# A new order table for a fused attention and channel-mix kernel: first transfers, prices of landing and storing, and the stores ahead of the branch

## The chip, the core and the metric

The program runs on one core of a Trainium2 chip. The metric is the device time of one execution in microseconds (us); less is better. The core's engines work side by side, each through its own list of instructions in order: TensorE (PE in the profile; PEld is its weight load), VectorE (DVE), ScalarE (ACT), GpSimd (POOL) and SyncE (SP), which here only issues transfers. Waits between engines are semaphores. Transfers are issued by SP and, in a few places, by ACT.

## What is computed

Linear attention with softmax over features, then a channel mix with a gate. Cut to what matters:

```python
# q, k, v: (8 batches, 8 heads, 576, 64)
q_s = softmax(q, axis=-1)
k_s = softmax(k, axis=2)                       # over the sequence
kv  = einsum('bhsd,bhse->bhde', k_s, v)
x   = einsum('bhsd,bhde->bhse', q_s, kv)       # then (B, S, H*D) = (8, 576, 512)

x_prev = x shifted by one position, zeros in front
xk = mu_k * x + (1 - mu_k) * x_prev
xr = mu_r * x + (1 - mu_r) * x_prev
k  = maximum(xk @ w_k, 0)                      # w_k: 512 x 1024
v  = (k * k) @ w_v                             # w_v: 1024 x 512
out = sigmoid(xr @ w_r) * v                    # w_r: 512 x 512
```

## The kernel before

**Work.** A batch's eight heads are taken in two halves u = 0, 1 of four heads; `q b.u`, `k b.u`, `v b.u` are its loads (0.59 MB each). The steps of a batch, with the engine that runs them:

- `exp` of q and k on ACT (L332), cast of v to bf16 (L238), mostly on POOL; `sum_q` and `scale_q` on DVE (L342 to L347) normalise q.
- q is transposed: for batches 0 and 1 by TensorE (`turn_q`, L361), its result taken out of PSUM by two evictions; for later batches by a DMA transpose (L369).
- `kv` (L378) and, for batches 0 and 1, weighting by mu (`weigh_kv`, L393) and eight mixing steps `x_mixed` (L410), each evicted by ACT or DVE, that give xk and xr directly. For later batches `x` (L432), `shift_x` on ACT (L440) and `mix_x` on DVE (L445).
- `up b.f`, f = 0 to 7 (L454): xk times one eighth of w_k; `relu` on ACT (L459); `square` of a pair on DVE (L469) or ACT (L467).
- Two batches i = 0 to 3 together have nine tiles m of 128 rows: `gate i.m` (L473), `tanh` on ACT (L478), `down i.m` (L490), `finish` on DVE (L496) and `store` (L506), which issues two transfers, one for each half of the rows.

All three weights come in as f32 and are cast to bf16: w_k in two transfers (1.05 MB each) and eight casts, w_r in one transfer and two casts on POOL, w_v in two transfers and four casts. Every gate needs both casts of w_r, every `down` all four of w_v. The mixing weights mu are spread over the partitions by two small matmuls (`spread_mu`) and kept by ACT (`keep_mu`) and DVE (`keep_cols`).

**Order.** The order is set by a planner and a table. Each piece of work is a numbered step with an engine, a cost, a latency (`lat`, from its end to when others see it) and its predecessors. The table `ORDER` lists all 709 step numbers; a letter A, D or G puts a step with a choice of engines on ACT, DVE or POOL. `Plan.run` goes through the table, gives each step a start from the costs, and picks a buffer for each tile (the one that is free first by the plan). `Plan.emit` emits the steps by planned start; so each engine's list is the table cut down to that engine, and the costs decide only buffers, the merging of engines, and warm-up matmuls: `emit` fills TensorE's planned idle time from 2.0 us up to the step `up 0.0` with matmuls on the identity (L320), which keep its clock up. SP's list holds loads, DMA transposes and stores in one line, so a store that waits for its `finish` holds up what is behind it.

**The branch.** Softmax is computed without subtracting the maximum. A check of all row sums (`watch`, `gather`, `judge`, `read_flag`) decides on a branch (L793) whether a safe version of everything is computed again. The branch stands ahead of `down 3.7`, `down 3.8` (in two halves of the columns, a and b) and the finishing and storing of three tiles, 3.6, 3.7 and 3.8 (`TAIL`). All else is issued ahead of it. `landed` is a step without an instruction: it stands for the landing of all stores outside the tail. Of the tail's stores, both halves of 3.6 and the second halves of 3.7 and 3.8 are issued by ACT, the others by SP.

**Tiles on chip.** The loads have three buffers of each kind, `ot` (a tile's output) has four, the tail's outputs three; PSUM holds three two-bank buffers (`two`: transposes, kv, mixing, `up`) and two one-bank buffers (`one`: gate, down).

Of the kernel before, what the change touches and what calls it, by code (L numbers as in the profile page):

```python
# [18 lines left out]


ORDER = """
0 7 8 9 10 11 12 13 14 19 1 2 24 28 76 96 3 4 80 81 100 82 6 79G 77 84A 78G 101 83A 85 5 102 97
86 90 91A 87 98G 99G 103D 105 94 104D 95A 88 106 107 108 89A 110 112 109D 111A 113D 114 115D 17G
92 93D 27 18G 21D 367 368 22D 365 366 15A 29 20G 26 370 30 16D 31 23D 372 33 32 377 371 373 25
369D 536 136 378 116 375 34 537 374D 140 141 120 376 121 362 119G 360 526 117 531 361 527 118G
125 139G 363 137 532 142 122 124A 126 127 143A 521 123D 138G 145 37 40 43 130 144D 131A 134 146
148 135A 147 150 149A 151D 35G 128 154 129A 364D 152 153D 379D 38G 39D 41 380 155A 36G 42 45 381
522 156 397 159 387 382 383 160 388 173 46 161 523 524 176 385 386 157 389A 384D 44 177 538 539
528 158 398 529 162 163 132 133A 190 193 395 392 551 178 393 175 49 396 399D 552 530 533 174 194
534 164 561 165 390 166 541 167 170 55 48 192 391 562 179 47 168 546 169 180 394D 540 181 542  # L30
547 556 563 171 186 187 557 172 182 188 50 548 183 241 184 195 185 207 415 416 407 51 189 549
408 210 211 212 417 405 191 52 410 209 418 406 409A 196 564 411 576 197 400 208 244 565 245 577
535 402 401 403 571 198 419D 200 213 56 199 572 53 543 214 412 413 558 404D 550 201 202 204 57
544 414D 203 559 205 206 215 217 566 216 218 567 54 221 568 220 578 246 219 222 242 223 224 243
427 428 569 437 225 425 227 420 426 228 226 429D 247 545 438 421 581 430 431 579 586 582 58 587
248 249 251 230 250 231 591 229 592 422 252 553 423 255 583 254 570 253 257 258 232 580 59 560
256 237 435 238 584 233 436 64 554 573 424D 240 61 601 66 60 239 234 259 65 235 432 236 62 574
433 260 261 262 63 602 442 452 596 575 439D 443 275 440 441 606 292 450 453 294 278 434D 597 447
279 455 444D 295 263 608 585 451 293 280 264 456 607 298 299 555 277 609 448 525 265 445 276 598
266 446 449D 267 599 281 67 611 282 68 268 270 612 269 610 272 588 589 621 283 271 73 273 274 69  # L40
622 289 593 288 296 590 297 284 457 603 290 285 286 458 287 75 291 462 472 309 463 310 604 459D
626 594 595 470 627 473 74 471 467 616 311 454A 468 465 345 343 312 313 460 461 346 314 466 347
628 629 300 617 70 469A 301 315 316 302 304 305 303 344 613 614 475 615 646 306 72 647 308 476
71 464D 477 641 605 642 307 618 478 474D 479D 317 323 349 619 319 636 348 637 350 638 322 324
318 320 321 639 643 325 620 485 326 328 329 487 488 486 495 644 327 482 496 330 640 623 483 624
351 357 332 356 333 352 651 652 653 353 666 667 359 645 497 358 498 480 354 331 481 492 630 355
499D 656 654 334 648 657 649 600 650 335 336 493 337 340 338 633 661 339 341 662 490 491 489D
494D 342 631 632 512 655 513 484A 671 672 500 634 510 511 517 658 659 660 501 502 503 504A 518
668 505 506 691 704 705 515 514D 516 692 669 676 507 681 670 706 707 625 677 682 673 519D 674
675 663 508 509D 678 664 679 680 665 635 683 684 686 687 696 688 697 520 689 685 708 690 693 694  # L50
701 695 702 703 698 699 700
"""


# [88 lines left out]
def kernel(  # L143
# [397 lines left out]
    def dma(cost, fn, after=(), uses=(), lat=2.0):  # L541
        return pl.step("DMA", cost, fn, after=after, uses=uses, lat=lat)
# [11 lines left out]
    def ld(n, b, u, after=()):  # L554
        cost = 2.4 if b + u == 0 and n != "v" else 1.53 if b < 2 else 1.55
        ev["ld", n, b, u] = dma(cost, lambda: load(n, b, u), after=after,
                                uses=[sl("ld" + n, b, u)], lat=2.2 if b < 3 else 2.6)
        return ev["ld", n, b, u]

    def ld_half(b, u, h, after=()):  # L560
        ev["ld", "v", b, u, h] = dma(0.77, lambda: load("v", b, u, (h, h + 1)), after=after,
                                     uses=[sl("ldv", b, u)], lat=2.2)
# [13 lines left out]
    for a, b in zip(queue, queue[1:]):  # L576
        pl.link(b, [a])
    first = [ld(n, 1, u, queue[-1:]) for n, u in (("q", 0), ("q", 1), ("k", 0), ("v", 0), ("k", 1))]
    first += [ld_half(1, 1, h, queue[-1:]) for h in range(2)]
    ev["wv"] = []  # L580
    for a in range(2):
        first.append(dma(2.75, lambda a=a: load_wv(a), uses=[sl("k2", "w")],
                         after=[*queue[-1:], *(ev["wk", i] for i in range(FT))]))
# [92 lines left out]
    for i in range(B // 2):  # L676
        for m in range(J):
            bs = [b for b in (2 * i, 2 * i + 1) if (m <= 4 if b == 2 * i else m >= 4)]
            s, th, ot = sl("one", "rp", i, m), sl("th", i, m), sl(kept(i, m), i, m)
            p = pl.step("PE", T_GATE, lambda i=i, m=m: gate(i, m),  # L680
                        after=[*ev["wr"], *(ev["mix", b, u, 1, c] for b in bs for u in range(2)
                                            for c in range(2))],
                        uses=[sl("xr", i), s, th], lat=0.2)
            t = pl.step("ACT", 0.52, lambda i=i, m=m: tanh(i, m), after=[p], uses=[s, th])
            squares = [ev["sq", b, f] for b in bs for f in range(FT // 2)]
            for a in ((None,) if (i, m) != LAST else (0, 1)):
                s, z = sl("one", "vp", i, m, a), 1.0 if a is None else 0.5
                late = [branch] if (i, m) in TAIL else []
                ev["down", i, m, a] = p = pl.step(
                    "PE", z * T_DOWN, lambda i=i, m=m, a=a: down(i, m, a),  # L690
                    after=[*ev["wv"], *squares, *(late if (i, m) != TAIL[0] else [])],
                    uses=[sl("k2", i), s], lat=0.2)
                ev["fin", i, m, a] = f = pl.step(
                    "DVE", 0.6 * z, lambda i=i, m=m, a=a: finish(i, m, a),
                    after=[p, t, *late], uses=[s, th, ot])
                ev["store", i, m, a] = o = dma(0.75 * z, lambda i=i, m=m, a=a: store(i, m, a),
                                               after=[f], uses=[ot])
                if late:
                    f["tail"] = o["tail"] = True
                    p["tail"] = (i, m) != TAIL[0]  # L700
            ev["th", i, m] = t
# [127 lines left out]
```

## Time and profile before

| | us |
|---|---|
| median of 3 runs (201.13 to 202.19) | 201.28 |
| the profiled execution's own time | 200.41 |
| its span on the core | 198.5 |
| TensorE busy (1908 matmuls) | 187.5 (94%) |
| VectorE busy | 148.1 (75%) |
| ScalarE busy | 139.6 (70%) |
| GpSimd busy | 31.3 (16%) |
| mean granted TensorE clock | 0.985 |

The span runs from the core's first instruction to its last; the time has some 1.9 us around it. A timeline row has start, duration, engine, line, operation, output and inputs, a count where neighbours are merged, and in brackets the idle time before it and what ended it. Rows of SPq and ACTq are issues of transfers; a transfer lands later (an output store 2.2 to 8.0 us after its issue, 2.9 in the median).

### The profile page before, as it was taken

Reading aid. Unit: us, or ns where it says so; the run is one execution under the profiler, and the core shown is the slowest. Engines: PE = TensorE matmul, PEld = TensorE weight load, DVE = VectorE, ACT = ScalarE, POOL = GpSimd, SP = SyncE. Lnnn points to the kernel's source line nnn. Section 1 sums busy time; section 2 is a strip of 40 time slices with the busy share of each in tenths; the row PEclk is TensorE's granted clock in tenths of the full one; section 3 lists DMA queues with packets and bytes.
Section 4 is the critical chain, followed back from the end, with each engine's and each line's share of the span. In section 5 each row is a group of like instructions: output and inputs, shape, how many; then the busy total and the mean of one; then the engine's idle time right before and its main releaser. Section 6 shows DMA issues by size and latency. Waiting matters only on the chain. (4 is left out here: it accounts for less than half of the span.)

```text
span 198.5 us, 4750 instructions
## 1 busy us (share of the span) xinstructions
PE 187.5 (94%) x1908; PEld 113.8 (57%) x1932; DVE 148.1 (75%) x230; ACT 139.6 (70%) x206; POOL 31.3 (16%) x43
## 2 busy tenths in 40 slices
PE   6699999999999999999999999999999999999990
PEld 4466865756546754654666546755574657564450
DVE  1978699999898999966999799799696474524230
ACT  3574699778999969968879687997857667452200
POOL 2073514622002300400016002300200000000000
PEclk9889999999999999999999999999999999999997
DMA  5999999989999499978999899984948022151555
GB/s 206 359 397 387 391 390 390 388 300 204 260 345 278 106 275 345 267 163 218 386 396 262 191 342 275 290 198 101 310 116 192 14 55 54 42 118 33 117 129 154
DMA packets 35897, 46.88 MB, mean 236 GB/s; under 512 B 16280, under 2 KB 16544, under 8 KB 35872
## 3 DMA queue, kind: packets, MB, share of 16 engines
q1 hardware_dynamic: 35456, 46.02, 78.2%
q10 hardware_dynamic: 416, 0.53, 1.0%
q8 instruction: 16, 0.26, 0.6%
q14 instruction: 9, 0.07, 0.1%
HBM read 33.56 MB, written 9.44 MB: 217 GB/s over the span
## 5 line engine op out<-in xcount | busy, mean ns | idle before, releaser
L454 PE MATMUL two<-xk,wk_bf 128*128 128x288 bf16 x512 | 68.0, 286 | 0.0
L490 PE MATMUL one<-wv_bf,k 128*128 128x512 bf16 (+1 forms) x283 | 65.1, 373 | 1.1 <-PEq L793 0.4
L454 PEld LDWEIGHTS <-wk_bf 128*128 128x128 bf16 x512 | 49.7, 98 | 17.6
L459 ACT ACTIVATE rel<-two 128x576 bf16<-128x576 f32 x64 | 40.5, 652 | 21.3 <-PE two L454 21.1
L490 PEld LDWEIGHTS <-k 128*128 128x128 bf16 x296 | 28.6, 98 | 31.0 <-issue 0.6
L238 POOL CAST vb<-ldv 128x1152 bf16<-128x1152 f32 (+1 forms) x20 | 22.3, 1131 | 101.0 <-DMA ldv<-in_v_dram 101.0
L473 PE MATMUL one<-wr_bf,xr 128*128 128x512 bf16 x133 | 35.7, 379 | 0.8 <-issue 0.3
L440 ACT ACTIVATE aw<-two,om 128x575 bf16<-128x575 f32 x48 | 32.9, 746 | 5.0 <-PE two L432 5.0
L496 DVE SCALAR_TENSOR_TENSOR ot<-th,one 128x512 f32<-128x512 f32 x33 | 22.3, 680 | 14.5 <-PE one L490 14.4
L478 ACT ACTIVATE th<-one 128x512 f32<-128x512 f32 x36 | 21.4, 600 | 12.9 <-PE one L473 12.7
L469 DVE TENSOR_TENSOR k<-rel 128x1152 bf16<-128x1152 bf16 x26 | 21.7, 839 | 5.0 <-ACT rel L459 5.0
L342 DVE TENSOR_REDUCE rs<-eq 128x18 f32<-128x1152 bf16 x16 | 21.5, 1346 | 2.1 <-ACT eq L332 2.1
L445 DVE SCALAR_TENSOR_TENSOR xk<-two,mu,aw 128x576 bf16<-128x576 f32 x24 | 19.3, 812 | 4.5 <-ACT aw L440 3.9
L347 DVE TENSOR_TENSOR qs<-eq,inv 128x1152 bf16<-128x1152 bf16 x16 | 22.3, 1396 | 0.3
L445 DVE SCALAR_TENSOR_TENSOR xr<-two,mu,aw 128x576 bf16<-128x576 f32 x24 | 19.3, 810 | 2.5 <-ACT aw L440 2.5
L332 ACT ACTIVATE eq<-ldq 128x1152 bf16<-128x1152 f32 x16 | 18.5, 1168 | 2.3 <-DMA ldq<-in_q_dram 2.3
L473 PEld LDWEIGHTS <-xr 128*128 128x128 bf16 x144 | 13.2, 98 | 11.6 <-issue 0.2
L332 ACT ACTIVATE ek<-ldk 128x1152 bf16<-128x1152 f32 x16 | 18.8, 1172 | 1.1 <-DMA ldk<-in_k_dram 1.1
L320 PE MATMUL one<-ident 128*128 128x256 bf16 x58 | 10.5, 330 | 1.8 <-DVE halves L258 1.8
L320 PEld LDWEIGHTS <-ident 128*128 128x128 bf16 x58 | 6.3, 120 | 4.1 <-DVE halves L258 1.8
L378 PEld LDWEIGHTS <-ek 64*64 64x64 bf16 x576 | 6.2, 107 | 3.2 <-ACT rel L459 1.3
L378 PE MATMUL two<-vb,ek 64*64 64x65 bf16 x576 | 7.7, 194 | 0.2 <-POOL vb L238 0.2
(54 smaller groups left out, 86.3 us busy)
## 6 DMA issues: line engine op xcount, KB each, us to landing
ldq<-in_q_dram SPq DMA_DIRECT2D x16, 576.0 KB, 6.6
ldk<-in_k_dram SPq DMA_DIRECT2D x16, 576.0 KB, 7.4
out_dram<-ot SPq DMA_DIRECT2D x66, 128.0 KB, 3.3
ldv<-in_v_dram SPq DMA_DIRECT2D x14, 576.0 KB, 9.2
k<-in_moe_w_k_dram SPq DMA_DIRECT2D x2, 1024.0 KB, 11.3
k<-in_moe_w_v_dram SPq DMA_DIRECT2D x2, 1024.0 KB, 13.7
ldv<-in_v_dram SPq DMA_DIRECT2D x4, 288.0 KB, 11.0
xr<-in_moe_w_r_dram SPq DMA_DIRECT2D x1, 1024.0 KB
```

The source lines that it names most:

```text
L238: return {"DVE": nc.vector, "POOL": nc.gpsimd}[eng].tensor_copy(out=out, in_=in_)
L332: nc.scalar.activation(out=at("e" + n, b, u)[:].rearrange("p j (h d) -> p h j d", h=2), in_=at("ld" + n, b, u)[:].rearrange("p h (j d) -> ...
L342: nc.vector.reduce_sum(out=rs[:], in_=at("eq", b, u)[:].rearrange("p j (h d) -> p (j h) d", h=2), axis=AX.X)
L347: nc.vector.tensor_tensor(out=at("qs", b, u)[:].rearrange("p j (h d) -> p (j h) d", h=2), in0=at("eq", b, u)[:].rearrange("p j (h d) -> p ...
L440: nc.scalar.activation(out=at("aw", b, u, h, w)[:, 1:S], in_=x_of(b, u, h)[:, 1:S], func=ACT.Copy, scale=om[:, c:c + 1])
L445: nc.vector.scalar_tensor_tensor(out=blend(b, w)[:, 2 * u + h, :], in0=x_of(b, u, h)[:, 64:64 + S], scalar=mu[:, c:c + 1], in1=at("aw", b, ...
L454: nc.tensor.matmul(ps[:, a, 0:HS], lhsT=wk_bf[:, ct, 128 * f:128 * f + 128], rhs=xk[:, ct, HS * a:HS * a + HS], start=(ct == 0), stop=(ct ...
L459: nc.scalar.activation(out=at("rel", b, f // 2)[:, f % 2, :].rearrange("p (a c) -> p a c", a=2), in_=at("two", "up", b, f)[:, :, 0:HS], fu ...
L469: nc.vector.tensor_tensor(out=dst, in0=r[:], in1=r[:], op=ALU.mult)
L473: nc.tensor.matmul(at("one", "rp", i, m)[:], lhsT=at("xr", i)[:, ct, 128 * m:128 * m + 128], rhs=wr_bf[:, ct, :], start=(ct == 0), stop=(c ...
L490: nc.tensor.matmul(at("one", "vp", i, m, a)[:, cols], lhsT=at("k2", i)[:, f, 128 * m:128 * m + 128], rhs=wv_bf[:, f, cols], start=(f == 0) ...
L496: nc.vector.scalar_tensor_tensor(out=at(kept(i, m), i, m)[:, cols], in0=at("th", i, m)[:, cols], scalar=1.0, in1=at("one", "vp", i, m, a)[ ...
```

## The change

Two things change: the prices and links that the planner works with, and the table. The steps are the same 709, with the same numbers; no instruction is added to or taken out of the steps' functions.

```diff
-    ev["mup"] = p = pl.step("PE", 2.2, spread_mu, after=[p],
+    ev["mup"] = p = pl.step("PE", 1.4, spread_mu, after=[p],
...
     def ld(n, b, u, after=()):
-                                uses=[sl("ld" + n, b, u)], lat=2.2 if b < 3 else 2.6)
+                                uses=[sl("ld" + n, b, u)], lat=3.0 if b else 2.2)
...
-    queue = [ld("q", 0, 0), ld("q", 0, 1), ld("k", 0, 0), ld("v", 0, 0), ld("k", 0, 1),
+    early = [ld("q", 0, 0), ld("q", 0, 1), ld("k", 0, 0), ld("v", 0, 0), ld("k", 0, 1),
              ld_half(0, 1, 0), ld_half(0, 1, 1)]
+    for a, b in zip(early, early[1:]):
+        pl.link(b, [a])
+    queue = []
     for a in range(2):
-        queue.append(dma(2.85, lambda a=a: load_wk(a), uses=[sl("k2", "w")]))
+        queue.append(dma(2.85, lambda a=a: load_wk(a), after=early[-1:], uses=[sl("k2", "w")]))
...
-    queue.append(dma(2.85, load_wr, uses=[sl("xr", "w")]))
+    queue.append(dma(2.85, load_wr, after=early[-1:], uses=[sl("xr", "w")]))
...
-    for a, b in zip(queue, queue[1:]):
-        pl.link(b, [a])
-    first = [ld(n, 1, u, queue[-1:]) for n, u in (("q", 0), ("q", 1), ("k", 0), ("v", 0), ("k", 1))]
-    first += [ld_half(1, 1, h, queue[-1:]) for h in range(2)]
+    first = [ld(n, 1, u, early[-1:]) for n, u in (("q", 0), ("q", 1), ("k", 0), ("v", 0), ("k", 1))]
+    first += [ld_half(1, 1, h, early[-1:]) for h in range(2)]
...
-                ev["store", i, m, a] = o = dma(0.75 * z, lambda i=i, m=m, a=a: store(i, m, a),
-                                               after=[f], uses=[ot])
+                ev["store", i, m, a] = o = dma(0.6 if late else 0.75 if i < 2 else 1.25,
+                                               lambda i=i, m=m, a=a: store(i, m, a), after=[f],
+                                               uses=[ot])
...
-    for t in ((*TAIL[1], None), (*LAST, 0), (*LAST, 1)):
-        pl.link(ev["store", *t], [landed])
+    pl.link(branch, [landed])
```

So the weights and batch 1's loads, which had a fixed order (w_k, w_k, w_r, then batch 1), are now only behind batch 0's loads, in whatever order the table has. The branch, not the tail's stores, is now planned behind the landing of the other stores. All lines of the table change; read by the steps' names, what the two tables hold at both ends is:

```text
SP, after batch 0's loads
  before  wk wk wr | q1.1 q1.0 k1.0 v1.0 k1.1 v1.1 | wv wv | q2.0 q2.1 k2.0
  after   wk q1.1 wk q1.0 wr k1.0 v1.0 k1.1 v1.1 | wv wv | q2.0 q2.1 q3.0

casts of weights
  before  POOL wk 2 3 4, wr 1 0, wv 0 2 1;  ACT wk 0;    DVE wk 5 6 1 7, wv 3
  after   POOL wk 0 3 1 7 5 6, wr 1 0, wv 2 1;  ACT wk 2 4;  DVE wv 3 0

TensorE, batch 0 and 1 (xm = x_mixed)
  before  .. 8 xm 0 | up 0.3 .2 .4 .5 .7 | gate 0.3 | up 0.6 .1 .0 | gate 0.1 0.2
          | kv 1.0 turn 1.1 1.0 | gate 0.0 | kv 1.1 | 7 xm 1 | up 1.0 .7 .3 .1 | down 0.0
  after   .. 7 xm 0 | up 0.0 .1 .3 .2 .7 .6 .4 | xm | up 0.5 | turn 1.1 | gate 0.1
          | turn 1.0 | gate 0.3 | kv 1.0 | gate 0.0 0.2 | 2 xm 1 | kv 1.1 | 5 xm 1
          | up 1.3 .2 .7 .0 | down 0.0

TensorE, the end
  before  .. down 3.3 3.1 3.4 3.5 | gate 3.6 3.8 | down 3.6 | BRANCH | down 3.7 3.8b 3.8a
  after   .. down 3.2 3.4 3.5 3.0 | gate 3.7 3.8 3.6 | down 3.6 | BRANCH | down 3.8a 3.7 3.8b

stores, the end
  before  .. 3.0 3.2 2.2 3.3 3.4 3.1 2.4 3.5 | BRANCH | 3.6 3.7 3.8b 3.8a
  after   .. 3.3 2.4 2.7 3.1 2.6 3.2 2.3 3.4 3.5 3.0 | BRANCH | 3.8a 3.6 3.7 3.8b

squares on ACT instead of DVE
  before  1.1 2.1 4.2 5.1 6.0 7.0        after  0.1 0.2 1.0 1.1 2.0 4.2 4.1 5.0 6.2 6.1 7.1
```

In batch 0, `keep_mu` also moves ahead of the exponential of k0.0 on ACT, `keep_cols` ahead of `sum_q 0.1` on DVE, and the evictions of q0.1 from DVE to ACT.

More of the change, by code (lines that the diff above doesn't have):

```diff
@@ L28 @@
[L28 to L33, printed above, removed]
@@ L46 @@
[L46 to L51, printed above, removed]
+0 1 2 3 7 76 4 8 80 81 9 96 10 11 78G 79G 6 12 13 14 5 82 100 101 77 85 83A 86 102 28 99G 98G
@@ new lines @@
+15G 84A 19 27 24 97 29 88 18G 16G 87 30 105 103A 106 89A 104A 31 107 90 91A 92 108 109A 93D 33
+110 111D 23G 94 17A 112 136 360 95D 362 32 361 20A 21G 113D 22G 363 34 140 367 365 141 368 377
+366 116 375 376 370 120 378 369A 114 115D 121 372 142 143D 26 364D 373 117 25 526 527 118D 122
+371 124D 37 40 43 46 536 144D 119G 537 125 521 137 126 123D 138A 531 130 139G 128 127 145 379D
+131A 129A 38G 134 146 147 148 135A 150 151D 149A 152 374A 153D 522 154 41 42 387 36G 158 532 388
+385 155D 39D 156 386 397 44 35D 380 159 381 160 161 398 523 382 395 45 524 175 173 176 177 178
@@ new lines @@
+47 528 538 396 190 157 392 529 383 132 384A 539 174 540 50 162 133A 49 399D 533 530 389A 163 193
+393 551 552 164 165 534 390 194 166 167 391 561 562 55 170 541 179 542 48 168 169 546 180 181
+183 547 394D 182 171 172 186 563 564 184 192 187 51 548 188 185 556 189 191 400 207 401 195 412
+210 413 535 241 557 405 407 410 211 212 576 408 196 406 57 415 411 209 577 549 550 417 244 414D
+59 416 565 402 409D 208 418 197 245 571 403 572 213 198 214 199 419D 558 52 200 56 54 201 202
+543 204 404A 559 203 544 215 205 216 246 581 582 217 219 566 218 578 567 568 221 220 222 224 53
@@ new lines @@
+206 545 223 420 421 427 579 430 242 431 428 227 425 432 228 426 437 243 580 247 433 434D 248 569
+586 66 225 249 438 255 226 230 229 254 570 58 583 429D 231 422 584 61 585 251 64 256 257 62 250
+587 423 253 553 554 555 259 232 238 252 591 65 573 60 424D 237 435 233 239 294 240 592 601 63
+234 235 258 236 452 436 574 439D 602 275 453 447 596 261 262 597 606 448 292 260 607 263 445 450
+278 451 279 440 446 454A 560 293 455 295 442 456 608 443 280 449A 298 525 264 609 265 299 277
+598 266 441 599 276 281 267 611 575 268 282 269 270 588 589 73 612 67 69 272 311 621 271 68 283
@@ new lines @@
+622 284 296 274 616 288 289 600 617 603 273 297 291 457 285 290 593 458 286 75 345 343 309 604
+462 460 444D 287 461 463 464A 590 459D 312 470 313 471 74 472 473 474D 465 594 595 626 627 467
+466 477 478 346 347 468 646 469D 628 647 310 314 300 302 315 629 316 306 618 619 641 475 305 610
+308 613 71 301 304 344 70 642 307 303 476 479D 317 323 614 349 636 322 637 324 605 643 319 318
+350 320 638 487 72 488 321 495 326 490 644 325 491 492 620 496 348 639 329 327 615 493 623 494A
+351 356 328 330 357 332 333 624 359 353 651 482 652 352 640 483 653 355 358 331 631 632 480 656
@@ L52 @@
+654 354 671 481 672 655 497 334 657 498 666 336 485 335 340 484D 338 633 499D 667 337 486 634
+625 489A 339 648 673 341 342 507 508 704 674 512 513 500 505 506 510 675 511 676 705 677 509A
+515 706 635 516 661 662 502 663 517 649 650 503 681 664 665 501 514D 518 519D 707 645 668 504D
+669 670 630 682 678 683 679 658 680 684 691 692 659 685 660 708 696 697 686 688 687 520 689 698
+699 700 693 690 694 695 701 702 703
 """
@@ L561, in ld_half @@
         ev["ld", "v", b, u, h] = dma(0.77, lambda: load("v", b, u, (h, h + 1)), after=after,
-                                     uses=[sl("ldv", b, u)], lat=2.2)
+                                     uses=[sl("ldv", b, u)], lat=3.0 if b else 2.2)
         return ev["ld", "v", b, u, h]
-    queue = [ld("q", 0, 0), ld("q", 0, 1), ld("k", 0, 0), ld("v", 0, 0), ld("k", 0, 1),
+    early = [ld("q", 0, 0), ld("q", 0, 1), ld("k", 0, 0), ld("v", 0, 0), ld("k", 0, 1),
              ld_half(0, 1, 0), ld_half(0, 1, 1)]
+    for a, b in zip(early, early[1:]):
+        pl.link(b, [a])
+    queue = []
     for a in range(2):
-        queue.append(dma(2.85, lambda a=a: load_wk(a), uses=[sl("k2", "w")]))
+        queue.append(dma(2.85, lambda a=a: load_wk(a), after=early[-1:], uses=[sl("k2", "w")]))
         for c in range(4):
@@ L582 @@
         first.append(dma(2.75, lambda a=a: load_wv(a), uses=[sl("k2", "w")],
-                         after=[*queue[-1:], *(ev["wk", i] for i in range(FT))]))
+                         after=[*queue, *(ev["wk", i] for i in range(FT))]))
         for c in (2 * a, 2 * a + 1):
```

18 lines of the change are left out of this document (removed).

## The prediction

> **What bounds the kernel now.** I read the slices first, then the waits, then the timelines of the two ends.
>
> ```profile
> PE   6699999999999999999999999999999999999990
> DMA  5999999989999499978999899984948022151555
> ```
>
> Share of each fortieth of the span, in tenths. TensorE is full from the third slice to the end; the DMA engines are full for the first eight slices (40 us), so the head is fed by one saturated stream of transfers.
>
> ```profile
> PE one L320 <- DVE halves L258: 1.8, 1, 1.8
> PE two L361 <- DVE qs L347: 1.5, 1, 1.5
> PE one L490 <- PEq L793: 0.4, 1, 0.4
> PE two L410 <- ACT xk L237: 0.4, 2, 0.2
> ```
>
> TensorE's longest waits. The first two lie before the first `up`, the third is the branch. Between 36 and 189 us nothing longer than 0.2 us is listed: TensorE does its matmuls back to back. The change moves no matmul out of the program, and from `down 0.0` on the two tables hold the same TensorE steps with the same number (8) of narrow steps next to each other. So the middle can only stay or get worse, and a gain must come from before `down 0.0` or behind the last matmul.
>
> ```profile
> 19.67 5.06 PE L454 MATMUL two<-xk,wk_bf 128*128 128x288 bf16 x40
> 24.57 0.49 PE L320 MATMUL one<-ident 128*128 128x256 bf16 x3
> 36.80 4.09 PE L454 MATMUL two<-xk,wk_bf 128*128 128x288 bf16 x32
> 40.73 1.89 PE L490 MATMUL one<-wv_bf,k 128*128 128x512 bf16 x7
> ```
>
> TensorE's order in time: first `up` at 19.67, batch 1's first `up` at 36.80, `down 0.0` at 40.73.
>
> ```profile
> 15.93 1.17 POOL L238 CAST wk_bf<-k 128x512 bf16<-128x512 f32 x2 [1.98 <-DMA k<-in_moe_w_k_dram]
> 21.89 2.55 POOL L238 CAST wr_bf<-xr 128x1024 bf16<-128x1024 f32 x2 [2.10 <-DMA xr<-in_moe_w_r_dram]
> 31.20 1.48 POOL L238 CAST vb<-ldv 128x576 bf16<-128x576 f32 x2 [1.05 <-DMA ldv<-in_v_dram]
> 37.27 2.55 POOL L238 CAST wv_bf<-k 128x1024 bf16<-128x1024 f32 x2 [1.65 <-DMA k<-in_moe_w_v_dram]
> 38.84 1.52 DVE L238 CAST wv_bf<-k 128x1024 bf16<-128x1024 f32 x1
> ```
>
> POOL stands waiting for transfers: these starts are landings. The last cast of `w_v` ends at 40.36, 0.37 us before `down 0.0`.
>
> ```profile
> 185.24 6.25 SPq L506 DMA_DIRECT2D out_dram<-ot  x8
> 189.88 3.77 PE L490 MATMUL one<-wv_bf,k 128*128 128x512 bf16 x24 [0.36 <-PEq L793]
> 192.26 3.40 ACTq L506 DMA_DIRECT2D out_dram<-last  x5
> 193.62 1.77 SPq L506 DMA_DIRECT2D out_dram<-last  x3
> 193.69 0.42 DVE L496 SCALAR_TENSOR_TENSOR last<-th,one 128x256 f32<-128x256 f32 x1 [0.52 <-PE one L490]
> ```
>
> The tail. SP has eight store issues in a row until 191.49, takes the branch, and starts the tail's stores only at 193.62; ACT starts its own at 192.26. Both are still issuing 1.3 to 1.6 us after the last `finish` ended at 194.11.
>
> **Part 1, the order of transfers.** The bytes ahead of `w_v` are the same, only permuted, so its second half still lands at about 37.2. What moves is `w_r`: it changes places with q1.1 and q1.0. The bytes up to and with `w_r` are now those that were ahead of and with q1.0, which landed at 25.78 (issue 12.65, 13.13 to landing), against 21.84 for `w_r` before. `w_k`'s second half moves behind q1.1 (0.59 MB; neighbouring landings of that size lie 1.5 us apart): 19.1 to about 20.6.
>
> **Part 2, casts and evictions.** Six casts of `w_k` go to POOL, two to ACT and none to DVE (before: three, one, four); two of `w_v` go to DVE (before: one). ACT takes eleven squares instead of six. I walk the head with the durations of the rows. `keep_mu` (four ACT operations, 1.16) moves into ACT's wait before k0.0 (1.05 idle at 8.70), so the exponential of k0.1 starts as it lands, 0.4 earlier; the two evictions of q0.1 leave DVE (0.81). `kv 0.0` stays at 12.76 (it waits for POOL's cast of v0.0). With three PSUM buffers handed on eviction by eviction, the last blend for `up 0.0` ends at about 18.1 and `up 0.0` starts at 18.3 instead of 19.67, with one mixing step (0.42) put off: 1.0 us ahead.
>
> That lead is not kept. `up 0.6` is the sixth of the eight: its cast is POOL's third after the landing at 20.6, and `scale_q 1.1` (1.36) falls between them: 23.9, a stall of 0.6. The eighth `up` ends at 27.3, `turn_q 1.1` at 27.95. `gate 0.1` needs both casts of `w_r`: 25.83 + 2 x 1.04 = 27.9, just in time. `turn_q 1.0` waits for `scale_q 1.0`, which the cast holds back to 27.9 to 29.25: stall 0.4. `kv 1.0` then waits for DVE's half of v1.0 (31.1): stall 0.3. Two gates, and DVE's chain of evictions, weighting and one square (0.75), bring `kv 1.1` to 34.15 and batch 1's first `up` to 37.15, `down 0.0` to 41.1: **+0.35**. From below: `down 0.0` cannot start before the `w_v` casts, all four of which may now run behind the landing at 37.27: POOL 2 x 1.04, DVE 2 x 0.54 (what its 1.52 shows behind POOL's end at 39.82), one after the other, 40.43: **-0.3**. From above: see the third rival, **+1.0**. I take +0.35, the walk.
>
> The rows for taking turns: a POOL cast of 128x1152 takes 1.17 alone and 1.87 at 126.67, where DVE's `scale_q` runs until 127.52. The Trainium skill (SBUF — State Buffer, "SBUF: two separate sides") says VectorE and GpSimd share a port pair as an exclusive lock, held for the whole instruction; the trace agrees with 1.87 against 1.17. If they could run side by side, the four casts would end near 39.4 and the lower end would be about -0.9 instead of -0.3.
>
> **Part 3, the middle.** New prices of landing and storing change no instruction, only the order. Head-of-line on SP: counting TensorE work (0.98 an `up`, 0.865 a gate, 1.725 a `down`) between the `down` of a store and the first use of a load or transpose queued behind it, the tightest pair has 13.9 us before (store 2.6, transpose 7.0) and 14.4 after (store 1.2, transpose 4.0). The longest landing of an output store is 8.0 and a transpose took 4.9, so it is covered. **0**; above, as much as all of TensorE's short waits outside the first two, about 1.1 us; below, 0.
>
> **Part 4, the tail.** Before the branch SP now stores 3.2, 2.3, 3.4, 3.5, 3.0 instead of 3.4, 3.1, 2.4, 3.5 in one go, and one gate more lies between the last `down` ahead of the branch and the branch (three gates, 3 x 0.9, and `down 3.6`, 1.73). With two issues of 0.6 a tile against a `finish` every 1.73, SP issues the last of them 1.3 us after its `finish`, that is some 3 us before TensorE reaches the branch, instead of 1.6 after it (191.49 against 189.88). SP then waits for landings at the branch (2 us, 191.5 to 193.6 before), and is through before the first tail store is ready. ACT's five issues no longer start late: 3.8's first half and 3.6 are issued while TensorE does 3.7, and the last two halves go out as `finish` ends. The last issues started at 194.84 (SP) and 195.10 (ACT), 0.73 and 0.99 behind the last `finish`; they will start at once. **-0.85**, between -0.7 and -1.0. TensorE's time behind the branch stays: the same three pieces, the halves of 3.8 now around 3.7, the last `finish` still a half tile (0.42). If SP were late again, all of this goes.
>
> `spread_mu` at 1.4 instead of 2.2 lets more warm-up matmuls in behind it; none lies on the path. `landed` has no instruction.
>
> **Sum** against the profiled execution: 200.41 (span 198.5, 1.9 around it) + 0.35 - 0.85 = 199.9. The runs' median is 201.28, 0.87 above that execution; the same -0.5, rounded to -0.55 for the three warm-up matmuls at 24.57 that now end with the first `up`, gives 200.7.
>
> **The rivals.** Half a per cent, what can be told from no change, is 1.0 us: 200.27 to 202.29.
>
> *Both ends pay.* The walk is late by a semaphore here and there, and `down 0.0` starts on its casts: -0.3 - 0.9 = **200.1**. For it: TensorE is ready 1 us earlier at the first `up`, and only 0.65 of slack is missing. Against: every step of DVE between 26 and 35 is in the way.
>
> *The port takes one more turn.* If `scale_q 1.0` gets in front of `w_r`'s second cast (they ask within 0.15 us of each other by the walk), the cast ends at 29.25, `gate 0.1` starts 1.3 later, part of it taken up by the waits behind it: `down 0.0` at 41.7, +1.0; with the tail **201.5**.
>
> *The clock falls (slower).* Warm-up matmuls are only filled in up to `up 0.0`, which before was the eighth `up` of its batch and is now the first. The stalls before `gate 0.1`, `turn_q 1.0` and `kv 1.0` (0.7 to 2 us together) are bare.
>
> ```profile
> 7.00:8.00 1.00, 0.23 (x3) 0.00 (x0) 0.95 (x2) 0.64 (x1) 0.00 (x0) 1.00 1.03 387
> 9.00:10.00 1.00, 1.00 (x11) 0.94 (x9) 0.97 (x2) 0.95 (x2) 0.00 (x0) 0.50 1.02 403
> ```
>
> Per stretch: TensorE's busy time is the second number, the granted clock the third from the end. About 1.1 us idle between 4.7 and 8.1 was followed by a clock of 0.5 for 3.41 us. If the stalls add up to more than about 1.1 us in one such stretch, 3.41 us run at half speed: 1.7 lost. With +1.0 to +1.4 in the head and -0.85 in the tail: **203.0**. Against: the stalls at 33 to 36 (some 0.9) left the clock at 1.00. The Trainium skill (TensorE: Matmul & The Clock Gate, "Why this matters for your kernels") asks for idle gaps over about 3 us before the clock falls; by that it would not happen here, but the row shows it after far less.
>
> *The tail's order does nothing.* SP's branch still waits past the last `finish`: +0.35 alone, **201.6**.
>
> **Chances.** Forecast (200.2 to 201.1) 0.38; both ends 0.27; one more turn 0.12; clock 0.19; tail does nothing 0.04. Faster by more than 0.5%: all of both ends and about a fifth of the forecast's: 0.35. Slower: the clock's 0.19 and a little of the port's: 0.21. The rest, 0.44, is within. The range goes from a little below both ends (199.8) into the clock case (202.8).
>
> **What would show it.** First `up` near 18.3; `gate 0.1` near 28 with a stall before it or `turn_q 1.0`; `down 0.0` between 40.4 and 41.7; TensorE without waits from there; SP's stores through before the branch, the tail's last issues within 0.1 us of the last `finish`, 4.39 from there to the span's end shrunk to 3.5. Wrong: a granted clock under 1.00 between 25 and 40, a new wait of TensorE in the middle, or tail stores still in a queue.

## The result and the profile after

The changed kernel takes 199.86 us in the median of 20 runs (199.03 to 201.32), the kernel before 201.43 (20 runs, 199.40 to 203.02): ratio **0.9941**, 95% interval 0.9917 to 0.9964, that is 1.2 us less (0.7 to 1.7). The profiled execution after took 199.3 us with a span of 197.5, before 200.41 with 198.5. One profiled execution further below, that of before_again (203.19), counts as a slow one: its lengths are shown, but they stand in no mean.

The slices of the page after:

```profile
PE   6999998899999999999999999999999999999991
DMA  5999999999999499798999799669923120426735
```

TensorE now dips a little in the seventh and eighth slice (30 to 40 us, the waits of the head) and is full to the end. TensorE's waits, longest in total first (engine, operation's output and line, what it waited for: us in total, times, longest):

```profile
PE one L320 <- DVE halves L258: 1.8, 1, 1.8
PE one L473 <- issue: 0.5, 3, 0.2
PE two L410 <- ACT xk L237: 0.5, 2, 0.3
PE two L454 <- DVE xk L238: 0.3, 1, 0.3
PE two L378 <- ACT rel L459: 0.2, 1, 0.2
```

The 1.5 us wait of the first transpose is gone from the list, and small waits of the head (L454, L378) have come in; those of L410 went from 0.4 to 0.5 in all. TensorE's timeline through the head (start, duration, engine, line, operation, output and inputs; idle time before it in brackets):

```profile
18.91 7.03 PE L454 MATMUL two<-xk,wk_bf 128*128 128x288 bf16 x56
27.73 1.03 PE L473 MATMUL one<-wr_bf,xr 128*128 128x512 bf16 x3
30.32 0.48 PE L378 MATMUL two<-vb,ek 64*64 64x65 bf16 x36 [0.20 <-ACT rel L459]
36.50 4.08 PE L454 MATMUL two<-xk,wk_bf 128*128 128x288 bf16 x32 [0.34 <-DVE xk L238]
40.42 1.89 PE L490 MATMUL one<-wv_bf,k 128*128 128x512 bf16 x7
```

First `up` at 18.91, seven of the eight without a gap, first gate at 27.73, batch 1's first `up` at 36.50 and `down 0.0` at 40.42: 0.31 earlier than before. POOL's timeline shows the landings:

```profile
20.41 1.73 POOL L238 CAST wk_bf<-k 128x512 bf16<-128x512 f32 x3 [2.96 <-DMA k<-in_moe_w_k_dram]
24.61 2.03 POOL L238 CAST wr_bf<-xr 128x1024 bf16<-128x1024 f32 x2 [2.46 <-DMA xr<-in_moe_w_r_dram]
36.04 2.03 POOL L238 CAST wv_bf<-k 128x1024 bf16<-128x1024 f32 x2 [5.38 <-DMA k<-in_moe_w_v_dram]
```

`w_r` is there at 24.6, not 25.8, and `w_v`'s second half at 36.0. The tail, from the timeline of the last 12 us:

```profile
185.92 1.88 SPq L506 DMA_DIRECT2D out_dram<-ot  x3
191.14 3.04 SPq L506 DMA_DIRECT2D out_dram<-last  x3
191.14 3.35 ACTq L506 DMA_DIRECT2D out_dram<-last  x5
192.34 0.69 DVE L496 SCALAR_TENSOR_TENSOR last<-th,one 128x512 f32<-128x512 f32 x1 [1.24 <-PE one L490]
193.22 0.42 DVE L496 SCALAR_TENSOR_TENSOR last<-th,one 128x256 f32<-128x256 f32 x1 [0.19 <-PE one L490]
```

SP is through with the stores ahead of the branch at 187.8, 5.8 us before the last `finish` ends (193.64), and its tail issues start when a `finish` ends. ACT's five issues run in one block from 191.14 to 194.49; the last one starts 0.29 behind the last `finish`.

### The profile page after: what moved, and what is told of

Its sections match the earlier page's. It is cut to its first block, busy times and chain, and to the rows that moved or that the text cites. A ratio compares the mean times of both kernels' runs of the same rounds, so it can differ in the third digit from the quotient of the medians.

```text
span 197.5 us, 4764 instructions
## 1 busy us (share of the span) xinstructions
PE 188.2 (95%) x1908; PEld 114.1 (58%) x1933; DVE 144.3 (73%) x225; ACT 145.3 (74%) x211; POOL 28.1 (14%) x43
## 5 line engine op out<-in xcount | busy, mean ns | idle before, releaser
L454 PE MATMUL two<-xk,wk_bf 128*128 128x288 bf16 x512 | 67.0, 286 | 0.3 <-DVE xk L238 0.3
L454 PEld LDWEIGHTS <-wk_bf 128*128 128x128 bf16 x512 | 49.7, 98 | 17.0 <-issue 0.7
L473 PE MATMUL one<-wr_bf,xr 128*128 128x512 bf16 x131 | 34.8, 379 | 1.0 <-issue 0.5
L238 POOL CAST vb<-ldv 128x1152 bf16<-128x1152 f32 (+1 forms) x18 | 19.5, 1092 | 102.0 <-DMA ldv<-in_v_dram 68.5
L469 DVE TENSOR_TENSOR k<-rel 128x1152 bf16<-128x1152 bf16 x21 | 17.1, 821 | 2.3 <-ACT rel L459 2.2
L467 ACT ACTIVATE k<-rel 128x1152 bf16<-128x1152 bf16 x11 | 12.8, 1166 | 0.2
L378 PEld LDWEIGHTS <-ek 64*64 64x64 bf16 x576 | 6.1, 107 | 3.0 <-ACT rel L459 2.2
## 6 DMA issues: line engine op xcount, KB each, us to landing
xr<-in_moe_w_r_dram SPq DMA_DIRECT2D x1, 1024.0 KB, 13.5
```

What stands on the lines that cost most here:

```text
L238: return {"DVE": nc.vector, "POOL": nc.gpsimd}[eng].tensor_copy(out=out, in_=in_)
L454: nc.tensor.matmul(ps[:, a, 0:HS], lhsT=wk_bf[:, ct, 128 * f:128 * f + 128], rhs=xk[:, ct, HS * a:HS * a + HS], start=(ct == 0), stop=(ct ...
L473: nc.tensor.matmul(at("one", "rp", i, m)[:], lhsT=at("xr", i)[:, ct, 128 * m:128 * m + 128], rhs=wr_bf[:, ct, :], start=(ct == 0), stop=(c ...
```

## The experiments

Twelve kernels ran, in three groups. Each run's ratio is against the kernel before, run on the same chip beside it. From each profile three lengths are read: when `down 0.0` starts (the head), from there to the end of the last `finish` (the middle), and from there to the span's end (the tail). All in us:

| kernel | ratio [95%] | `down 0.0` | middle | tail |
|---|---|---|---|---|
| before | | 40.73 | 153.38 | 4.41 |
| before_again (before once more) | 0.9989 [0.9958, 1.0021] | 41.33 | 155.53 | 4.55 |
| b_mu14 (four warm-up matmuls more) | 1.0011 [0.9976, 1.0046] | 40.57 | 154.59 | 3.93 |
| t_stores (two stores moved) | 0.9952 [0.9921, 0.9982] | 41.90 | 154.50 | 3.27 |
| h_head_after (new head, old rest) | 1.0013 [0.9984, 1.0041] | 39.85 | 154.70 | 3.89 |
| m_v (two loads moved) | 0.9981 [0.9953, 1.0009] | 41.06 | 153.84 | 4.45 |
| m_v3 (three loads moved) | 0.9974 [0.9938, 1.0010] | 41.04 | 153.47 | 4.40 |
| h_m (new head, three loads moved) | 0.9956 [0.9924, 0.9987] | 41.03 | 153.48 | 3.85 |
| b_two (two stores, three loads moved) | 0.9905 [0.9871, 0.9940] | 40.78 | 153.59 | 3.27 |
| after | 0.9941 [0.9917, 0.9964] | 40.42 | 153.22 | 3.87 |
| after_again (after once more) | 0.9928 [0.9900, 0.9955] | 40.83 | 153.23 | 4.03 |
| h_head_before (old head, new rest) | 0.9950 [0.9916, 0.9984] | 42.03 | 153.92 | 3.83 |
| e_v_back (after, one load put back) | 0.9914 [0.9879, 0.9950] | 41.00 | 153.22 | 3.88 |
| e_first (after, one store moved) | 0.9879 [0.9844, 0.9915] | 40.90 | 153.22 | 3.60 |

**First group: which end pays.** The two tables were cut at `down 0.0` and joined crosswise, and the tail's part was tried in the old table by itself.

> The kernel before once more, to see how much of its profile repeats. If the late landing of its transfers belongs to the program, the second half of w_v lands within 0.3 us of 37.2 and down 0.0 starts near 40.7; if it is chance, the landing lies nearer the 36.0 of the changed kernel. The tail repeats in any case: the last finish ends about 4.4 us before the span does, and the last issue of a tail store starts 0.7 to 1.0 us behind that finish. Ratio 1.000.

The second half of `w_v` is there at 36.37 this time, so its landing is chance; yet `down 0.0` starts at 41.33, later than in before, so that landing does not set it. The tail repeats: 4.55, the last issue 1.18 behind the last `finish`.

> The changed kernel's table up to down 0.0, the table before for all that is left. Theory (head and tail are separate terms): first up near 18.9, down 0.0 near 40.4, no TensorE wait behind it, the tail of before with 4.4 us behind the last finish; span 0.3 less than before's, ratio 0.997 to 1.000. Rival (the head gives most of the gain): ratio 0.995 or less.

> The table before up to down 0.0, the changed table for all that is left. Theory: first up near 19.7, down 0.0 near 40.7, the changed tail with 3.8 us behind the last finish; span 0.6 to 0.8 less than before's, ratio 0.996 to 0.998. Rival (the head gives most of the gain): ratio 0.998 or more.

```diff
 h_head_after: ORDER up to "down 0.0"
-  as before
+  as in the changed table; then the old table's remaining steps, with the old link of `landed`
 h_head_before: ORDER behind "down 0.0"
-  as before
+  the changed table's remaining steps, with its link of `landed`
```

h_head_before also keeps the changed price of `spread_mu`, and so has four warm-up matmuls more, as b_mu14 below.

The new head with the old rest is not faster (1.0013), although its profile shows `down 0.0` 0.9 earlier; the old head with the new rest has 0.9950, about all of the gain. So by the times the gain is behind `down 0.0`. The expectation for h_head_after missed twice: TensorE waits 1.1 us in the middle of h_head_after, and its tail, with the old stores, is 3.89 instead of 4.4. For the stores alone, in the old table:

> The kernel before with only SP's list changed: stores 2.4 and 3.1 ahead of 3.4. Theory (SP's backlog delays the tail): SP reaches the branch near 188.2 instead of 191.5, the tail's last issue starts within 0.1 us of the last finish, from there to the span's end 3.5 us instead of 4.4; span 0.7 to 0.9 less than before's, ratio 0.995 to 0.997. Rival (the tail waits for landings or the branch itself): SP's issues start as late as before, change under 0.2 us.

```diff
 SP, the end
-  3.0 3.2 2.2 3.3 3.4 3.1 2.4 3.5 | BRANCH
+  3.0 3.2 2.2 3.3 2.4 3.1 3.4 3.5 | BRANCH
```

Nothing but SP's list differs. Two rows of its timeline show the tail's issues:

```profile
192.94 4.00 ACTq L506 DMA_DIRECT2D out_dram<-last  x5
194.89 2.01 SPq L506 DMA_DIRECT2D out_dram<-last  x3
195.98 0.42 DVE L496 SCALAR_TENSOR_TENSOR last<-th,one 128x256 f32<-128x256 f32 x1 [0.52 <-PE one L490]
```

SP's last issue and ACT's last issue both start within 0.03 of the last `finish` (it ends at 196.41), and the tail is 3.27. By the times, two stores out of their place cost 1.0 us before (0.4 to 1.6), as the prediction said of the tail. What they cost is not the same in each execution: in before, m_v and m_v3 the last issue starts 0.97 to 1.07 behind the last `finish` (tail 4.40 to 4.45), in b_mu14, h_head_after and h_m, with the same order of stores, only 0.46 to 0.59 (3.85 to 3.93).

**What hides in the old middle.** In the profiled execution of before TensorE waits for no `relu` in the middle. In the four others with the old table's middle and no load moved in it, it does: 1.5 and 0.3 us in before_again, 1.1 in t_stores, 1.1 in h_head_after, and twice about 0.5 in b_mu14. The rows around it, from the timeline of t_stores, in order of time:

```profile
102.88 1.36 DVE L347 TENSOR_TENSOR qs<-eq,inv 128x1152 bf16<-128x1152 bf16 x1
103.02 3.87 POOL L238 CAST vb<-ldv 128x1152 bf16<-128x1152 f32 x2 [18.46 <-DMA ldv<-in_v_dram]
104.16 1.71 DVE L469 TENSOR_TENSOR k<-rel 128x1152 bf16<-128x1152 bf16 x1
107.95 2.31 DVE L347 TENSOR_TENSOR qs<-eq,inv 128x1152 bf16<-128x1152 bf16 x1
110.96 0.65 ACT L459 ACTIVATE rel<-two 128x576 bf16<-128x576 f32 x1 [1.24 <-DVE k L469]
111.66 1.14 PE L454 MATMUL two<-xk,wk_bf 128*128 128x288 bf16 x8 [1.06 <-ACT rel L459]
```

POOL's casts of v start as the loads land. Two casts here take 3.87 instead of 2 x 1.17; VectorE's square takes 1.71 instead of 0.75 and `scale_q` 2.31 instead of 1.36, 0.96 and 0.95 longer, which is most of a cast of 1.17: each one stands still while a cast runs. The next square is then late; ACT's `relu` waits 1.24 for the buffer that it frees, and TensorE waits 1.06 for the `relu`. The same rows in the profiled execution of before:

```profile
101.71 1.36 DVE L347 TENSOR_TENSOR qs<-eq,inv 128x1152 bf16<-128x1152 bf16 x1
103.36 2.50 POOL L238 CAST vb<-ldv 128x1152 bf16<-128x1152 f32 x2 [18.94 <-DMA ldv<-in_v_dram]
103.65 1.34 DVE L342 TENSOR_REDUCE rs<-eq 128x18 f32<-128x1152 bf16 x1
105.21 1.25 DVE L469 TENSOR_TENSOR k<-rel 128x1152 bf16<-128x1152 bf16 x1
```

Here the casts land 1.65 us behind `scale_q`'s start, instead of 0.14, and run beside VectorE's sum of exponentials (the `TENSOR_REDUCE`), which is not held up; one square loses 0.5 and no wait of TensorE for a `relu` is listed. A difference of 1.5 us between a landing and VectorE's list decides on 1 us of TensorE.

**Second group: the loads of v, the tail's mending, the warm-up.**

> Before's kernel with two transfers moved in SP's list: the loads of v5.0 and v6.0 stand behind the DMA transpose of 4.0 (issue near 88 us) instead of behind the loads of q6.0 and q5.1 (near 93.6). Every other engine's list is before's. Theory: in three of four profiles of before's middle, POOL's casts of these loads start at 101.2 to 103.0, while VectorE's scale_q and squares run, and these take 1.71 to 2.31 us instead of 0.74 to 1.36; a square that is late holds ACT's relu, and TensorE waits 1.25 to 2.2 us near 108 to 111 us. With the loads 5 us earlier the casts start near 92 to 95, beside VectorE's f32 work, the wait is gone, down 0.0 to the last finish takes 153.2 to 153.6 us, and the median falls by about three quarters of 1.3, 1.0 us: ratio 0.995. Rival: the wait has another source (the transposes or the loads of q and k are late), or the profiled executions show it and the others do not: the wait stays or the median does not move, ratio 1.000.

> Before's kernel with three loads moved in SP's list: v5.0 and v6.0 behind the DMA transpose of 4.0 (as in the run with two), and v5.1 behind the load of k5.0 (issue near 90.6 instead of 96). All engines but SP and POOL have before's lists. With two loads moved, the third cast still started at 106.62 and made one square 1.71; the wait was down to 0.23 us and the middle 153.84. Theory: with all three casts over by 98 us, scale_q and the squares between 101 and 109 take 1.36 and 0.75, the middle (down 0.0 to the last finish) is 153.2 to 153.5, against 153.4 to 155.5 (mean 154.5) in five profiles of before's middle; ratio about 0.995. Rival: the middle's waits are no matter of most executions, ratio 0.998 to 1.000.

```diff
 SP, in the old table (m_v: without the last of the three moves)
-  turn 4.0, store 1.0 1.2, k5.0, store 0.7, q6.0 q5.1 v6.0 v5.0 k6.0 k5.1 v5.1
+  turn 4.0, v5.0 v6.0, store 1.0 1.2, k5.0, v5.1, store 0.7, q6.0 q5.1 k6.0 k5.1
```

With two loads moved, one collision is left (a square of 1.71 at 107.73), the middle is 153.84, and the ratio, 0.9981, lies nearer the rival's 1.000 than the 0.995 expected. With three moved, the casts are alone:

```profile
91.86 1.17 POOL L238 CAST vb<-ldv 128x1152 bf16<-128x1152 f32 x1 [5.57 <-DMA ldv<-in_v_dram]
93.97 1.17 POOL L238 CAST vb<-ldv 128x1152 bf16<-128x1152 f32 x1 [0.93 <-DMA ldv<-in_v_dram]
98.28 1.17 POOL L238 CAST vb<-ldv 128x1152 bf16<-128x1152 f32 x1 [3.14 <-DMA ldv<-in_v_dram]
102.11 1.36 DVE L347 TENSOR_TENSOR qs<-eq,inv 128x1152 bf16<-128x1152 bf16 x1
103.38 0.75 DVE L469 TENSOR_TENSOR k<-rel 128x1152 bf16<-128x1152 bf16 x1
106.23 1.34 DVE L347 TENSOR_TENSOR qs<-eq,inv 128x1152 bf16<-128x1152 bf16 x1
```

The cast is 1.17 three times, `scale_q` 1.36 and 1.34, the square 0.75, and TensorE has no wait over 0.2 in the middle: 153.47, and 153.48 and 153.59 in the two other kernels with these loads moved, h_m and b_two. The old middle has 154.29 in the mean of before, b_mu14, t_stores and h_head_after, 0.7 to 0.8 more. That is the mechanism in the profile. The times alone say it less clearly: 0.9974, with an interval that holds both the theory's 0.995 and the rival's 0.998 to 1.000. Three pairs differ in just these three loads: m_v3 against before -0.26%, h_m against h_head_after -0.57%, b_two against t_stores -0.47%. From the intervals (half widths squared and added) each pair is uncertain by 0.4 to 0.5%; their mean is -0.43%, 0.9 us, uncertain by 0.25%. That fits the profiles, and is too coarse to tell in what share of the executions the collision costs time.

> The changed kernel with one swap in ACT's list: store 3.6 (two issues) stands ahead of the second half of store 3.8a. Theory: in the changed kernel ACT's five tail issues run back to back from 191.14, 0.55 to 0.80 each, because the first of them waits for 3.8a's finish, though 3.6's finish had ended at 190.29; so the last starts 0.29 us behind the last finish. With 3.6 first, ACT starts 0.8 us earlier, its last issue starts within 0.05 us of the last finish, and the time from the last finish to the end falls from 3.87 to between 3.3 and 3.6: 0.3 to 0.5 us, which the ratio against before (0.994 to 0.992) can hardly tell. Rival: the landing of the last store sets the end whatever ACT does, 3.8 to 3.9 stays.

```diff
 ACT, behind the branch, in the changed table
-  3.8a (second half), 3.6 (both halves), 3.7 (second half), 3.8b (second half)
+  3.6 (both halves), 3.8a (second half), 3.7 (second half), 3.8b (second half)
```

```profile
190.80 4.14 ACTq L506 DMA_DIRECT2D out_dram<-last  x5
191.62 3.04 SPq L506 DMA_DIRECT2D out_dram<-last  x3
193.70 0.42 DVE L496 SCALAR_TENSOR_TENSOR last<-th,one 128x256 f32<-128x256 f32 x1 [0.18 <-PE one L490]
```

ACT now starts 0.82 ahead of SP, when 3.6 is ready, and its last issue starts 0.03 behind the last `finish` (194.12) instead of 0.29. The tail is 3.60, at the upper edge of the expectation, and this is the lowest ratio of all: 0.9879 against 0.9928 for the changed kernel beside it. The intervals overlap; the profile's share of the difference is 0.27 to 0.43 us of the 1.0.

> The changed kernel once more, beside the others on one chip. Theory (the new middle keeps POOL's casts away from VectorE's bf16 operations): no wait of TensorE over 0.6 us between down 0.0 and the branch, 153.0 to 153.9 us from down 0.0 to the last finish, where before's middle had 153.4, 154.5, 154.7 and 155.5; ratio 0.994. Rival (its middle is as exposed as the old one, and the profile taken was a lucky one): a wait of over 1 us shows up, 154.5 or more, and the gain comes from the head and the tail alone.

It came out as the theory had it: no wait over 0.3 in the middle, 153.23, ratio 0.9928. The other profiles with the new middle have 153.22 three times and, in h_head_before, 153.92, with waits of 0.3 and 0.2.

> Before's kernel with spread_mu priced at 1.4 instead of 2.2: four warm-up matmuls more on TensorE ahead of the first turn_q, nothing else. Theory: they are off the path, first up between 19.7 and 20.9 as in three profiles of before's head, ratio 1.000. Rival: they keep the clock up through the stretch where it was 0.50 in before (8 to 12 us), first up at 18.5 to 19.2, down 0.0 about 0.8 earlier, ratio 0.996.

```diff
-    ev["mup"] = p = pl.step("PE", 2.2, spread_mu, after=[p],
+    ev["mup"] = p = pl.step("PE", 1.4, spread_mu, after=[p],
```

No gain: 1.0011, first `up` at 19.51, though TensorE ran at full rate from 4.6 us on. The four warm-up matmuls are worth nothing that shows here; the rival's 0.996 lies outside the interval.

**Third group: why the new middle is safe, and whether the parts add.**

> The changed kernel with one load put back: that of v6.0 stands behind the load of k6.0, with v5.0's and v5.1's, as the old table has it, instead of ahead of the transpose of 4.0 (issue near 84.4). Theory: three casts of POOL then run one after the other from about 104, beside VectorE's scale_q at 105.0 and whatever bf16 work follows: one or two of these take 1.7 to 2.3 us, the middle grows from 153.2 by 0.3 to 1.2, ratio against before 0.995 to 0.998 instead of 0.993. Rival: the new middle is safe for another reason (squares 4.1 and 5.0 were moved to ACT, so that VectorE has less to do there), the middle stays at 153.2 to 153.4, ratio 0.993.

```diff
 SP, in the changed table
-  store 1.2, v6.0, turn 4.0, store 1.0, .. q6.0 k5.1, store 0.6, k6.0, v5.0 v5.1
+  store 1.2, turn 4.0, store 1.0, .. q6.0 k5.1, store 0.6, k6.0, v6.0 v5.0 v5.1
```

```profile
105.27 1.17 POOL L238 CAST vb<-ldv 128x1152 bf16<-128x1152 f32 x1 [23.55 <-PE two L454]
105.61 2.02 DVE L347 TENSOR_TENSOR qs<-eq,inv 128x1152 bf16<-128x1152 bf16 x1
106.75 3.02 POOL L238 CAST vb<-ldv 128x1152 bf16<-128x1152 f32 x2 [0.31 <-DMA ldv<-in_v_dram]
109.99 0.69 DVE L496 SCALAR_TENSOR_TENSOR ot<-th,one 128x512 f32<-128x512 f32 x1 [0.79 <-PE one L490]
```

The theory fell and the rival held. The collision is back (`scale_q` 2.02), but the middle stays at 153.22 and the ratio at 0.9914: VectorE has nothing urgent behind it and even stands idle for 0.79 soon after. In the new table VectorE has no square between 101 and 113 us, in the old one four; ACT does two there, at 106.34 and 109.51 (1.17 each). The place of the load isn't what makes the new middle safe; that VectorE has fewer such operations there fits, and was not tried by itself (squares on ACT in the old table).

> The new head (the changed table up to down 0.0) with the old rest, and in it the three loads of v moved as in the run beside it. The same kernel without the moves had ratio 1.0013 [0.9984, 1.0041] though its down 0.0 was at 39.85, 0.9 earlier than before's; its middle had a wait of 1.25. Theory A: the new head is 0.8 us earlier (down 0.0 at 39.9 to 40.9 in four profiles, 40.6 to 42.0 in six of the old head) and the collisions in the middle hid it: ratio 0.990 to 0.992, 0.4 per cent under the old head with the same moves. Theory B: in most executions the new head is worth nothing, or costs the 0.35 us of the walk: the same ratio as the old head with the same moves, or 0.002 more.

```diff
 SP, in the table of h_head_after
-  turn 4.0, store 1.0 1.2, k5.0, store 0.7, q6.0 q5.1 v6.0 v5.0 k6.0 k5.1 v5.1
+  turn 4.0, v5.0 v6.0, store 1.0 1.2, k5.0, v5.1, store 0.7, q6.0 q5.1 k6.0 k5.1
```

0.9956 against 0.9974 for the old head with the same moves lies between the two theories, with intervals wider than their distance. The profiles speak for B: `down 0.0` at 41.03 and 41.04. This kernel's middle is 153.48 without a wait, where the same kernel with the loads unmoved had 154.70.

> Before's kernel with five transfers moved in SP's list and nothing else: the three loads of v as in the run beside it, and the stores 2.4 and 3.1 ahead of 3.4 as in the run of the stores alone (0.9952). Theory: the two gains add, since the one lies at 102 to 111 us and the other behind the last finish (1.1 us each): ratio 0.989 to 0.990, as fast as the changed kernel with its tail mended (0.9879 [0.9844, 0.9915]), with the old head. Rival: what the middle saves is waited for again before the branch, ratio 0.995.

```diff
 SP, in the old table: both moves
-  turn 4.0, store 1.0 1.2, k5.0, store 0.7, q6.0 q5.1 v6.0 v5.0 k6.0 k5.1 v5.1
+  turn 4.0, v5.0 v6.0, store 1.0 1.2, k5.0, v5.1, store 0.7, q6.0 q5.1 k6.0 k5.1
...
-  3.0 3.2 2.2 3.3 3.4 3.1 2.4 3.5 | BRANCH
+  3.0 3.2 2.2 3.3 2.4 3.1 3.4 3.5 | BRANCH
```

0.9905: the two gains add, within the intervals (-0.48% and -0.26% alone, -0.95% together). Five transfers moved in SP's list bring the old kernel to where the whole new table brought it.

## Why the prediction was right and wrong

The forecast was 200.7, the result 199.86, 0.06 inside the lower edge of the range. That it is inside at all is luck: the edge was set by the rival in which both ends pay, and what paid beyond the forecast was the middle. Half of the gain was missed. In the profiled pair the sum of -1.11 is -0.31 in the head, -0.16 in the middle, -0.54 in the tail and -0.10 outside the span; the forecast had +0.35, 0 and -0.85.

- **The head's walk: order right, stalls too long, the sum of the wrong sign in the profiled pair.** First `up` 18.91 (forecast 18.3), first gate 27.73 (28.0), batch 1's first `up` 36.50 (37.15), `down 0.0` 40.42 (41.1). Three stalls were forecast, 0.6, 0.4 and 0.3. Measured in the changed kernel are none, none and 0.20. The first hung on `scale_q 1.1` getting in between POOL's casts of `w_k`. After, the three casts took 1.73 in all and `scale_q` waited for them instead (1.77 at 21.58); in e_v_back it went the forecast way (three casts 2.91) and the stall was 0.16; in after_again and h_head_after the casts took 2.86 too, and no `up` stalled. `w_r` landed 1.2 ahead of the estimate from the equal sum of bytes, which took the landing of q1.0 in one execution as fixed. In the six profiles with the new head `down 0.0` is at 39.85 to 41.03 (mean 40.67), in seven with the old one, before_again's left out, at 40.57 to 42.03 (mean 41.16). The times can't tell the heads apart: after and after_again against h_head_before give -0.2 and -0.4 us, h_m against m_v3 -0.4, h_head_after against before +0.3, each uncertain by 0.6 or more; their mean is -0.2. What the head is worth in the median stays open, between some half a us gained and a little lost.
- **The middle: the step that failed for the median.** That "the middle can only stay or get worse" was read off one execution in which TensorE had no wait for a `relu` there. That execution was 0.87 faster than the median, which the prediction wrote down and carried over unexplained. The middles of b_mu14, t_stores and h_head_after, with the same table there, are 1.1 to 1.3 us longer than before's, and the new table's is 153.22 or 153.23 in four profiles of five. The mark was there: a square of 1.25 instead of 0.75 and two casts in 2.50 instead of 2.34 in the profile of before. The prediction used the rule of taking turns for `w_k` and `w_r` and did not look for it in the middle, though the row it took the rule from, the cast of 1.87 at 126.67, lies there. The Trainium skill (SBUF — State Buffer, "SBUF: two separate sides") says that a VectorE operation with two SBUF inputs and a GpSimd operation that reads SBUF take the shared ports as an exclusive lock: the one that starts first has them for its whole instruction, and the other blocks. The traces agree: `scale_q` and square (two inputs) grow by 0.94 to 0.96 beside a cast of 1.17, while the sum of exponentials (one input) stayed at 1.34 beside the casts at 103.36 in before.
- **The tail: mechanism right, size off by 0.3.** SP is through long ahead of the branch's end, as forecast, and its last issue starts 0.03 behind the last `finish`. The forecast let ACT start its last issue at once too; but 3.6's two issues stand behind 3.8's first half in ACT's list, so that five issues of 0.6 to 0.8 ran in one block and the last was 0.29 late. The tail went from 4.41 to 3.87, and over all profiles from a mean of 4.16 (six with the old order, 3.85 to 4.45) to 3.90 (four, 3.83 to 4.03). So the 0.73 and 0.99 that the forecast took from before's rows as the lateness of the last issues are the late one of two cases. With ACT's list mended it is 3.60. In t_stores and b_two, whose last issues start no earlier, it is 3.27; where these 0.3 come from is open.
- **Together.** An estimate from these runs: head -0.2 (the mean above), middle -0.9 (the three pairs), tail -0.3 (4.16 to 3.90), -1.4 in all, against the measured -1.2 (-0.7 to -1.7).
- **The rivals.** Both ends paying gave 200.1, nearest to the time, but not for its reason: by the estimate above the middle paid the larger part. The clock didn't fall: no profile with the new head shows a granted clock under 1.00 between 13 and 186 us, although its three waits ahead of batch 1's first `up` (0.18, 0.27, 0.34) stand there as bare as was said. The price of that rival does not come out of its terms: 201.28 + 1.7 + 1.0 to 1.4 - 0.85 is 203.1 to 203.5, not 203.0; nothing else rests on it. The port's extra turn at `w_r` didn't come: its two casts took 2.02 or 2.03 together in all six. That the tail's order does nothing is refuted by t_stores.
- **The chances** followed from taking the middle as fixed: with 0.9 us in the middle given its due, the half per cent would have been passed by the forecast itself.

## What to carry to other kernels

One execution without a wait doesn't show that there is none: if it is faster than the median by more than the effect that is looked for, the difference has to be found before a stage is counted as free. Operations that run a little longer than their group's usual duration (here VectorE's two-input operations beside a POOL cast) mark where the next execution may stall; moving a load so that its cast lands in a quiet stretch cost nothing here. And behind a branch, each queue's list should have its transfers in the order in which their data get ready, on both queues, not just on the one that was late.

## What the runs showed of the hardware that was not expected

- A cast and a two-input VectorE operation don't slow each other down in part: who is first keeps its time (scale_q 1.36 at 102.88, the cast 0.14 behind it waiting), the other one grows by what is left, up to 0.96 on VectorE's side.
- TensorE's rate in the first 14 us differs between executions, also of one list of instructions. Read from the warm-up matmuls of 256 columns (start to start 213 ns at half, 109 ns at full rate), full rate begins at 4.6 to 4.7 us in before, b_mu14 and e_v_back, at 10.6 in after, by 7.1 in after_again, and at 13.5 in t_stores and h_head_before, though the granted clock of the slices reads 1.00 in after and t_stores all along. The two that were latest at full rate have the latest first `up`, 20.79 and 20.87, against 19.51 to 19.97 in the other six with the old head: some 1 us of head that goes with the execution and not with the table.
- Five of the fourteen profiles (before, before_again, m_v, h_m, e_first) then fall back to half rate for 3.41 us, between 8 and 13 us, and the fall comes 3.41 us after full rate began. In these 3.41 us TensorE stood idle for 0.95 to 1.53 us (1.10 in before, as the prediction read it); in b_mu14, h_head_after, after_again and e_v_back, which went on at full rate, for 0.63 to 0.83. But two of these stood idle for longer a little later, e_v_back for 1.44 us at 11.40 and b_mu14 for 1.31 at 11.31, and no fall followed: the idle time alone does not decide, and what else does is open.
- Landings of the same bytes vary as much: `w_r`'s first cast starts at 24.53 to 25.62 in the six new heads, `w_v`'s second half is there at 35.94 to 37.27 over all profiles.
